# Swapping two first loads between two queues, and a new hand-written order for the first 668 of 1502 steps, in a packed-attention and gated-convolution kernel

## The chip, the cores and the metric

One core of one Trainium2 chip runs the whole kernel. The metric is the device time of one execution in microseconds; lower is better. In the text PE is TensorE, DVE is VectorE, ACT is ScalarE, POOL is GpSimd and SP is SyncE, whose queue issues nearly all loads.

## What is computed

```python
def sm_attn(qq, kk, vv):
    s = scale * np.matmul(qq, kk.transpose(0, 1, 3, 2))
    a = np.exp(s - np.max(s, axis=-1, keepdims=True))
    a = a / (np.sum(a, axis=-1, keepdims=True) + 1e-09)
    return np.matmul(a, vv)
p_packed = sm_attn(p, k, v)               # 32 packed queries over 576 keys
out = sm_attn(q, p_packed, p_packed)      # 576 queries over the 32 packed rows
x = out.transpose(0, 2, 1, 3).reshape(8, 576, 512)
h = np.maximum(x @ w_in, 0.0)             # 512 -> 1024
conv_out = conv3(h, conv_w)               # depthwise, 3 taps along the sequence
return h * sigmoid(conv_out) @ w_out      # 1024 -> 512
```

There are 8 batches of 8 heads, 576 positions and a head width of 64. q, k, v and p are float32; w_in, conv_w and w_out come as float64 and are rounded to float32 on the chip.

## The kernel before

**Tiling.** Four heads of one batch are a group g, so there are 16 groups, two to a batch. For each group `attention(g)` is a chain of 21 steps: score of the packed queries (PE, step 0, L744), maximum (DVE), exp (ACT), transposes (PE, L894), their eviction `a1T`, product with v (PE, step 5, L902), scaling `pb` (ACT), a transpose and its eviction `ppT`, second score (PE, step 9, L744), then transpose, maximum, subtraction, exp, sum, reciprocal, product and transpose back (mostly DVE), and a split of the result into two parts, `hi` and `lo` (steps 19 and 20). `packed_weight(b, hf)` multiplies the packed rows with w_in (L1099). `ffn1(b, j)` for 8 slices j of the hidden width multiplies that with the attention weights (L1162, L1188), then come relu (ACT), the taps of the convolution, tanh and the gate (DVE and ACT, L1205 to L1247). `ffn2(m)` for 36 row tiles is the last product (L1315 in f32 for the first three tiles, L1368 in three products for the rest), eviction and store. The first two groups of both first batches have their keys and queries transposed on PE (`kT`, `qT`, L720) and evicted to SBUF; from group 4 on, a DVE transpose does that (L680).

**Loads.** `load_kq`, `load_v`, `load_weight` (eight tiles w0 to w7 of 1 MB) and `queries` (the packed queries: p0 in two parts, then p1 to p3) issue on SP's queue, in the order in which their steps stand. Keys of groups 0 to 3 come in runs of 4608 B; from group 4 on, in four DMAs of 128 B pieces (L660); p1 is four DMAs of 128 B pieces too (L855). Three transfers are issued by ACT instead: the first 640 columns of the first keys (L632), the rest of them and, before, the keys of group 1 (`more_keys`, L668 and L671). `hold` keeps SP's other loads back until the first of these has landed.

**Order.** `ORDER` is a string of two-digit stream numbers: `Flow.run` takes the next step of the named stream, so that it fixes the order on every engine. `Flow` holds a planner's costs; they decide nothing in the program but how many idle matmuls (`warm`, L298) are put on PE where the plan finds it empty, until the first step of `ffn2(2)` has been placed. `ON_DVE` and `ON_POOL` name the operations that go to DVE rather than ACT, and to POOL rather than DVE; `either`, `either_pool`, `copy` (L349 on DVE, L351 on ACT) and `tensor_tensor` (L341 on DVE, L344 on POOL) follow them.

Of the kernel before, what the change touches and what calls it, by code (L numbers as in the profile page):

```python
# [18 lines left out]


ORDER = (
    "007f3603076y34023636036y340504050a040506050a70057001343a066z05056z350c34050e36340534050c3b0h0c053b0d0505340c7672"
    "3b0h7209360c050b050505080d713c36050j3b0b0c0c710c0c0j0c05050j0l3d3q053q0g770c0j3q0c0o0k0c3d3q3e0c0i0j3d0o0i0c0c73"
    "3d73740c3s740c3f3q3t3g3q3q0c0c3f780c3t3s3s0f3q3h3f3s0m0n3t3t0k3f793h3u3s0q3t3i3r0j3r0q3t3h0s0q3r3s0r3u3t0j3r3u3u"
    "0r370j0j3s0q0j0q3t0j0q3k3u0q0p3t3u3s0z3s0p753j3h0q3v0q7a753j3u3w0q3v3r3w3j0j3j400j3m0q5y370q3w3u3r0q3v0v405z3r3u"
    "3v603w3r5z5y3x3l7b603l0j3v0q3x3l373v3o403l0j0x0q3x400j0t3w3w3v0q0j0j0q0x5z5y0q123y0x3n0j3y3w0j3y3x3n3y3x60600x7c"
    "3n3y3z0x3z3z5y0j3n1441143p0q410x163x3z0u0q5z413x0y3p60605y0q7d143y3p190y15423z1d5z5z101e3y3j3l421142433z413p0w42"
    "43433z420x425y4444443l4342435z433n1445455y0x3j144515433n46605y441y0x456046464438440x4561451b46446046140x1b14465z"
    "0x471b3p45605y474846476113141g3p494847486149485z491761141b1b49485y1k484747614949486147496161616118141i0x4a141i62"
    "611i621c4b1b62621462621c1j140x630x380x4a1i62621b1b3862141i1b0x624a1i0x1j631a1z0x5z1n1r1b0x62141p626414141p636363"  # L30
    "141f1b0x634b63631b141i4b14631l141i631b4c1b1p4c641b4c1u631q4d1p4d4e1p1i644c1b1h4c4e4d4c1i1q1w1p644d651w1b1m1w644c"
    "4d4e1i251s4d1b4f1i1p4e4d4e4e646364641i641p211w644e654f4g1b1i4f1o1b1i1x4h4f4g641t6565644h1i1i1b4h651w4g4k1p4h4f23"
    "4g4k1i1p1x231w1p4f66651w6565234h4g4f4h4h1w1w4k1i4g6523651i234i6565661i4i1p4i1v284i4j66664j4g4i4j4i2a4l1p1w231w2a"
    "662a4m4i4n4j4j1p4j661p664m664j66664o1w4n4m666724672a244m1p6861391p671p4n1p23674n674o2k23674l2a6767674m4l4m204m4o"
    "4n4p4o232c2b4n66674p4n4q671w262a68391w222f232b4q394p4o4u4q274q4o2j4o234q2a692h2h694q2m1w684u1p4q4p6868681w1p4r4p"
    "4r1w2h68684u682d68682i4s4p2h4s294r4s2a691w6969692a4p692h234t4t2e68694t4s4r69694r2o1w4s4v4t6a6a2o2a692q2h1w6a2i4s"
# [27 lines left out]
class Flow:  # L64
# [98 lines left out]
    def transfers(self, step, at):  # L163
        issue, delay = self.ISSUE[step.engine]
        issue = step.issue or issue
        slow = 0
        for _ in range(step.parts):
            if step.engine == "SP":
                at = max(at, self.flights.pop(0))
            at += issue  # L170
            if self.hiccup and self.data >= self.hiccup:
                self.data += 600
                self.hiccup = 0
                slow = 500
# [48 lines left out]
def tile_packed_attention_conv_gate(  # L223
# [29 lines left out]

    F64_REBIAS = 2.0**-112
    PE_LO = 2
    ON_DVE = {"gh510", "hi0", "hi1", "hi12", "kT00", "kT05", "kT25", "kT30", "qT00", "relu34", "relu76", "tap00", "tap01", "tap21", "tap40", "tap41", "tap42", "tap44", "tap46", "tap53", "tap56", "tap57", "tap60", "tap61", "tap64", "tap65", "tap67", "tap70", "tap72", "tap73", "tap74", "tap75", "tap77", "x140", "x180", "x230", "x270", "x280", "x310", "x340", "x90"}
    ON_POOL = {"add00", "add01", "add10", "add41", "add51", "add61", "add70", "add71", "lo0", "lo10", "lo11", "lo7", "mul10", "mul12", "mul14", "mul2", "mul3", "mul4", "mul5", "mul6", "mul7", "mul9", "sub10", "sub11", "sub15", "sub2", "sub3", "sub4", "sub5", "sub7", "sub8", "sub9", "xl100", "xl110", "xl280", "xl30", "xl320", "xl330", "xl350", "xl50", "xl60", "xl70", "xl80"}
    COLD = 7
    F1F = ()
    F2F = 3  # L260
# [335 lines left out]
    def load_v(g):  # L596
        b, gg = divmod(g, NG)
        yield Step(
            "SP",
            (2350 if g < 2 else 2200) if g < APART else 2800,  # L600
            after=held(g),
            take=["v"],
            sets=[("v", g)],
            parts=2 if g < APART else 1 + HG,
            late=(300 if g >= APART else 1500) * (g > 3),
            issue=620 * (g >= APART),
        )
# [13 lines left out]
        nc.sync.dma_start(out=t[128 - TAIL :, :, SV, :], in_=src[:, 128 * SV :].rearrange("h r d -> r h d"))  # L621

    def load_kq(g, name, src):
        b, gg = divmod(g, NG)
        if by_block(g):
            i = g + (NG if name == "q" else 0)
            after = ready("kT", i - 3) if g < NG and i >= 3 else []
# [9 lines left out]
            after = after + held(g)  # L637
            parts = HG if name == "q" and quad(g, "q") and g % NG else 1
# [819 lines left out]
```

## Time and profile before

| | |
|---|---|
| median of three runs | 393.4 us (393.32, 393.40, 395.52) |
| the profiled execution | 393.78 us |
| its span, first to last instruction | 391.8 us |
| granted TensorE clock, mean | 1.00 |

The 2.0 us between span and time lie around the first and the last instruction. All times in the rows are counted from the start of the span.

### The profile page before, as it was taken

What the parts mean: (1) busy time and instruction counts of PE and PEld (TensorE: products, weight loads), DVE (VectorE), ACT (ScalarE), POOL (GpSimd) and SP (SyncE); (2) the same over time, 40 slices, a digit from 0 to 9 for tenths busy, and PEclk for the clock granted to TensorE, in tenths of its full rate; (3) what the DMA queues carried; (4) which work ended last, traced back from release to release, by engine and by line L of the source; (5) the groups of instructions that cost most, each with busy time, mean ns of one, the idle gap of its engine ahead of it and who ended that gap; (6) DMA issues with size and microseconds to landing.
All of it is one profiled execution on the core that took longest, in us unless ns stands there. A gap on an engine that the chain in (4) does not pass through costs nothing.

```text
span 391.8 us, 8179 instructions
## 1 busy us (share of the span) xinstructions
PE 386.2 (99%) x3299; PEld 308.4 (79%) x3299; DVE 331.6 (85%) x494; ACT 245.0 (63%) x403; POOL 73.8 (19%) x58
## 2 busy tenths in 40 slices
PE   8999999999999999999999999999999999999996
PEld 7667665769678887878787897898797879898886
DVE  3699899999989999999999989799987897987010
ACT  2999989988658776675846364673546554444211
POOL 2140332202532442051120103000001100200420
PEclk9999999999999999999999999999999999999999
DMA  8999899989599808998555134001001100000211
GB/s 270 376 392 270 189 306 143 192 154 184 113 163 158 186 5 181 183 163 149 121 88 142 35 87 89 0 28 54 28 2 54 54 28 27 28 0 28 80 54 56
DMA packets 157542, 47.62 MB, mean 122 GB/s; under 512 B 145460, under 2 KB 148788, under 8 KB 157504
## 3 DMA queue, kind: packets, MB, share of 16 engines
q1 hardware_dynamic: 157040, 45.89, 49.6%
q10 hardware_dynamic: 432, 1.18, 0.8%
q8 instruction: 26, 0.43, 0.5%
q14 instruction: 12, 0.10, 0.1%
q0 software_dynamic: 32, 0.02, 0.0%
HBM read 37.64 MB, written 9.44 MB: 120 GB/s over the span
## 4 chain that ended last, share of the span: by engine, by line
PE 90%; DVE 4%; DMA 3%; ACT 1%; SPq 1%; issue 0%; ACTq 0%; DVEq 0%
PE fo L1368 41%; PE big L1188 24%; PE sm L1368 4%; PE big L744 4%; PE big L1315 4%; PE big L1099 3%; PE sm L902 2%; DMA k<-in_k_dram 2%; PE big L894 2%; PE fo L1315 2%; DMA hgt<-in_k_dram 1%; PE fo L1274 1%; PE sm L1274 1%; PE big L720 1%; DVE w_in_sb L341 1%; DVE tmp L459 0%
## 5 line engine op out<-in xcount | busy, mean ns | idle before, releaser
L1368 PE MATMUL fo<-wo_hi,xhi 128*128 128x512 f32 x232 | 93.4, 402 | 0.0
L1368 PE MATMUL fo<-wo_hi,xlo 128*128 128x512 f32 x232 | 90.8, 391 | 0.0
L1368 PE MATMUL fo<-wo_lo,xhi 128*128 128x512 f32 x232 | 90.5, 390 | 0.0
L1205 ACT ACTIVATE hbuf<-big 128x576 f32<-128x576 f32 x62 | 40.2, 654 | 46.3 <-PE big L1188 46.0
L1237 DVE SCALAR_TENSOR_TENSOR hgt<-hbuf,cw,hgt 128x576 f32<-128x576 f32 x64 | 53.4, 843 | 4.6 <-ACT hgt L1235 4.3
L1188 PE MATMUL big<-a2hi,ghi 128*128 128x288 f32 x244 | 55.3, 308 | 0.0
L1245 ACT ACTIVATE hgt<-hgt 128x576 f32<-128x576 f32 x64 | 43.4, 685 | 17.7 <-DVE hgt L1241 17.5
L1368 PEld LDWEIGHTS fo<-wo_hi,xhi 128*128 128x128 f32 x232 | 43.5, 188 | 11.2 <-issue 1.4
L1188 PE MATMUL big<-a2lo,ghi 128*128 128x288 f32 x244 | 52.3, 296 | 0.0
L1188 PE MATMUL big<-a2hi,glo 128*128 128x288 f32 x244 | 52.3, 295 | 0.0
L1241 DVE SCALAR_TENSOR_TENSOR hgt<-hbuf,cw,hgt 128x576 f32<-128x576 f32 x64 | 51.1, 810 | 0.5
L1368 PEld LDWEIGHTS fo<-wo_hi,xlo 128*128 128x128 f32 x232 | 43.6, 188 | 9.7
L1247 DVE SCALAR_TENSOR_TENSOR hgt<-hgt,hbuf 128x576 f32<-128x576 f32 x64 | 47.3, 752 | 3.2 <-ACT hgt L1245 2.8
L1368 PEld LDWEIGHTS fo<-wo_lo,xhi 128*128 128x128 f32 x232 | 43.6, 188 | 7.1
L1188 PEld LDWEIGHTS big<-a2hi,ghi 128*128 128x128 f32 x244 | 41.2, 189 | 6.2 <-issue 1.9
L344 POOL TENSOR_TENSOR xlo<-hgt,xhi 128x1024 fp32r<-128x1024 f32 x11 | 28.0, 2544 | 93.9 <-ACT xhi L351 38.2
L1383 ACT COPY o<-fo 128x512 f32<-128x512 f32 x30 | 17.5, 584 | 35.7 <-PE fo L1368 27.9
L1188 PEld LDWEIGHTS big<-a2lo,ghi 128*128 128x128 f32 x244 | 39.2, 189 | 0.0
L1188 PEld LDWEIGHTS big<-a2hi,glo 128*128 128x128 f32 x244 | 39.1, 188 | 0.0
L1235 ACT ACTIVATE hgt<-hbuf,cw 128x576 f32<-128x576 f32 x42 | 32.4, 777 | 2.8 <-DVE hbuf L1203 2.3
L344 POOL TENSOR_TENSOR s<-s,mx 128x576 f32<-128x576 f32 x10 | 14.3, 1434 | 102.2 <-DVE hgt L1241 58.5
L351 ACT CAST xhi<-hgt 128x1024 fp32r<-128x1024 f32 (+1 forms) x28 | 26.5, 952 | 9.2 <-PE fo L1368 4.0
(138 smaller groups left out, 609.1 us busy)
## 6 DMA issues: line engine op xcount, KB each, us to landing
out_dram<-o SPq DMA_DIRECT2D x35, 256.0 KB, 2.3
k<-in_k_dram SPq DMA_DIRECT2D x48, 144.0 KB, 3.6
q<-in_q_dram SPq DMA_DIRECT2D x48, 144.0 KB, 3.4
v<-in_v_dram SPq DMA_DIRECT2D x40, 128.0 KB, 3.0
v<-in_v_dram SPq DMA_DIRECT2D x6, 512.0 KB, 10.6
hgt<-in_moe_w_in_dram SPq DMA_DIRECT2D x3, 1024.0 KB, 11.8
hgt<-in_moe_w_out_dram SPq DMA_DIRECT2D x3, 1024.0 KB, 8.4
hgt<-in_q_dram SPq DMA_DIRECT2D x2, 576.0 KB, 7.0
```

Of the source, the lines that this page charges most:

```text
L344: added = nc.gpsimd.tensor_tensor(**kw)
L351: nc.scalar.copy(out=out, in_=in_)
L1188: nc.tensor.matmul(out=t[:, hf, :SH], lhsT=w[:, gg, js], rhs=x[:, hf * SH : (hf + 1) * SH], start=n == 0, stop=n == (1 if b in F1F else 3) ...
L1205: nc.scalar.activation(out=inner, in_=t[:, :, :SH], func=AF.Relu, scale=0.5)
L1235: nc.scalar.activation(out=d, in_=h[:, 1 : S + 1], func=AF.Copy, scale=cw[:, NJ + j : NJ + j + 1])
L1237: nc.vector.scalar_tensor_tensor(out=d, in0=h[:, 0:S], scalar=cw[:, j : j + 1], in1=d, op0=ALU.mult, op1=ALU.add)
L1241: nc.vector.scalar_tensor_tensor(out=d, in0=h[:, 2 : S + 2], scalar=cw[:, 2 * NJ + j : 2 * NJ + j + 1], in1=d, op0=ALU.mult, op1=ALU.add)
L1245: nc.scalar.activation(out=d, in_=d, func=AF.Tanh)
L1247: nc.vector.scalar_tensor_tensor(out=d, in0=d, scalar=1.0, in1=h[:, 1 : S + 1], op0=ALU.add, op1=ALU.mult)
L1315: nc.tensor.matmul(out=t, lhsT=src[:, c, :], rhs=w32[c // 2][:, c % 2, :], start=c == 0, stop=c == NJ - 1)
L1368: nc.tensor.matmul(out=t, lhsT=x[:, c, :], rhs=w[:, c % 2, :], start=c + i == 0, stop=c == NJ - 1 and i == 2)
L1383: nc.scalar.copy(out=o, in_=t)
```

## The change

**Two loads.** `K1_FIRST` becomes False. ACT's third transfer is now the queries of group 0 (576 KB) where it was the keys of group 1 (576 KB); the other one of the two goes on SP's queue.

**Order.** `ORDER` is replaced in its first 668 steps. The same steps stand there in another order, and the last 834 are equal. In it the loads come like this (k2 is the keys of group 2, and so on):

```
before  ACT: k0, rest of k0, k1
        SP:  p0a q0 v0 w0 k2 p0b q1 v1 w1 k3 q2 w2 w3 v2 v3 q3 w4 k4 p1 w5 k5 w6 w7 v4 k6 q4 ...
after   ACT: k0, rest of k0, q0
        SP:  p0a k1 k2 v0 p0b w0 q1 v1 w1 k3 w2 q2 w3 v2 p1 v3 w4 q3 w5 k4 w6 k5 w7 v4 q4 k6 ...
```

On PE, the first steps are (att0.5 is step 5 of `attention(0)`, pw `packed_weight`, p0a and p0b the packed queries' transposes, second halves of transposes left out):

```
before  kT0 p0a att0.0 qT0 kT1 att0.3 att0.5 att1.0 att0.7 att0.9 kT2 att1.3 p0b qT1 att2.0 att1.5 att1.7 att1.9
        pw0 att2.3 kT3 qT2 ffn1(0,0) ... att3.5 qT3 att3.7 ffn1(0,3) ffn1(0,4) att3.9 pw0 pw1 ffn2(0) ...
after   kT0 p0a qT0 att0.0 kT1 att0.3 att1.0 att0.5 kT2 att0.7 p0b att0.9 att1.3 att2.0 qT1 att1.5 att2.3 att1.7 att1.9
        pw0 kT3 att3.0 qT2 ffn1(0,0) ... att3.5 ffn1(0,3) ffn1(0,4) qT3 att3.7 ffn2(2) pw0 att3.9 pw1 ffn2(0) ...
```

**Engines.** From DVE to ACT go the evictions kT05, kT25 and kT30, the casts hi0 and hi1, and the taps tap01 and tap21; from ACT to DVE pT0, pT2, kT15, kT35, gh001, a1T2 and tap02 (the first digit is the group or batch). From DVE to POOL go add11, add31 (halves of the rounding of w1 and w3) and lo4; from POOL to DVE add41 and xl80.

**Planner.** Its costs of loads are set anew, and a load in small pieces now holds the planned queue.

```diff
+    AHEAD = 2100
...
+            if step.issue:
+                at = max(at, self.data - self.AHEAD)
...
-    K1_FIRST = True
+    K1_FIRST = False
...
+        yield Step("SP", ..., sets=[("wd", i)], late=600 * (i in (5, 6)))
...
-            late=(300 if g >= APART else 1500) * (g > 3),
+            late=(100 if g >= APART else 600) * (g > 3),
...
-        yield Step("SP", 3450, take=["kq"], sets=[(name, g)], parts=4, late=700, issue=830)
+        yield Step("SP", 3450, take=["kq"], sets=[(name, g)], parts=4, late=-100, issue=810)
...
-            late=0 if i < 2 else 2500,
+            issue=550,
+            late=900 * (i >= 2) - 300 * (i == 1),
```

## Rows read from the trace of the kernel before

**Rows 1.** Page, part 1: engine, busy us (share), instructions.

```profile
PE 386.2 (99%) x3299; PEld 308.4 (79%) x3299; DVE 331.6 (85%) x494; ACT 245.0 (63%) x403; POOL 73.8 (19%) x58
```

**Rows 2.** Busy time of each engine in six stretches, with clock and DMA.

```profile
core 0: us, PE busy (x) PEld busy (x) DVE busy (x) ACT busy (x) POOL busy (x), PEclk, DMA share, GB/s
4.43:27.31 22.88, 22.49 (x291) 15.31 (x291) 16.34 (x32) 17.12 (x35) 5.28 (x4) 1.00 1.04 377
27.31:43.28 15.97, 15.59 (x227) 12.52 (x226) 15.79 (x29) 15.97 (x28) 0.00 (x0) 1.00 0.91 240
43.28:68.49 25.21, 25.15 (x214) 13.40 (x214) 24.17 (x40) 23.25 (x35) 9.55 (x8) 1.00 0.97 229
68.49:98.34 29.85, 29.85 (x224) 22.97 (x222) 29.84 (x40) 27.33 (x44) 5.40 (x3) 1.00 0.95 176
98.34:149.18 50.84, 50.84 (x592) 39.85 (x599) 49.17 (x78) 35.98 (x63) 21.45 (x13) 1.00 0.66 132
149.18:391.77 242.59, 238.94 (x1753) 201.29 (x1737) 195.60 (x278) 124.08 (x201) 30.01 (x17) 1.00 0.30 68
```

**Rows 3.** Chain that ended last, unhindered steps: start us, us, line, matmuls.

```profile
169.03 0.70 PE sm L902 x40
169.73 0.65 PE big L744 x16
170.38 0.86 PE big L1099 x16
...
179.03 1.60 PE big L1188 x12
180.64 0.55 PE big L894 x5
```

**Rows 4.** PE's costliest lines in 4.43 to 27.31: the idle matmuls.

```profile
L298 PE MATMUL idle<-zeros 128*128 128x512 f32 x15 | 5.5, 443 | 0.0
```

**Rows 5.** DMA issues from 0.5 to 7.5 us: KB each, us to landing.

```profile
hgt<-in_k_dram ACTq DMA_DIRECT2D x1, 576.0 KB, 4.6
hgt<-in_q_dram SPq DMA_DIRECT2D x1, 576.0 KB, 3.9
...
hgt<-in_moe_w_in_dram SPq DMA_DIRECT2D x1, 1024.0 KB, 7.3
...
v<-in_v_dram SPq DMA_DIRECT2D x1, 512.0 KB, 5.7
```

**Rows 6.** Timeline of PE and POOL, 4 to 28 us: start us, us, what.

```profile
11.62 0.77 PE L902 MATMUL sm<-v,a1T 128*32 128x64 f32 x40
...
13.88 0.71 PE L744 MATMUL big<-qT,ppT 64*32 64x288 f32 x16
...
22.37 1.43 POOL L344 TENSOR_TENSOR a2lo<-a2t,a2hi 128x576 fp32r<-128x576 f32 x1 [0.56 <-DVE a2hi L349]
...
27.31 0.54 PE L1162 MATMUL big<-a2hi,ghi 128*128 128x288 f32 x2
```

**Rows 7.** DVE's groups by shape up to 100 us: operations that change engine.

```profile
L341 DVE CUSTOM_DVE_ANT_0 w_in_sb<-tmp 128x1024 uint16<-128x1024 uint16 x5 | 3.4, 689 | 0.0
...
L349 DVE COPY kT<-big 128x640 f32<-128x640 f32 x2 | 1.6, 820 | 4.2 <-PE big L720 4.2
...
L349 DVE COPY kT<-big 128x512 f32<-128x512 f32 x2 | 1.4, 682 | 0.0
L1231 DVE TENSOR_SCALAR hgt<-hbuf,cw 128x576 f32<-128x576 f32 x2 | 1.0, 522 | 0.0
L349 DVE CAST a2hi<-a2t 128x576 fp32r<-128x576 f32 x2 | 0.9, 460 | 0.1
```

**Rows 8.** Timeline of SP's queue, 29 to 44 us: issuing instructions.

```profile
29.36 11.56 SPq L660 DMA_DIRECT2D k<-in_k_dram  x4
40.97 2.20 SPq L855 DMA_DIRECT2D p<-in_p_dram  x4
43.27 0.43 SPq L418 DMA_DIRECT2D stage<-in_moe_w_out_dram  x1
```

**Rows 9.** Waits of DVE and ACT: us in total, times, longest.

```profile
DVE pT L861 <- DMA p<-in_p_dram: 1.0, 1, 1.0
...
ACT tmp L455 <- DMA stage<-in_moe_w_out_dram: 0.7, 1, 0.7
```

**Rows 10.** DMA issues from 40.9 to 43.7 us: KB each, us to landing.

```profile
p<-in_p_dram SPq DMA_DIRECT2D x4, 64.0 KB, 2.5
...
stage<-in_moe_w_out_dram SPq DMA_DIRECT2D x1, 1024.0 KB, 5.7
```

More of the change, by code (lines that the diff above doesn't have):

```diff
@@ L21 @@
 ORDER = (
[L22 to L31, printed above, removed]
@@ L32 @@
-    "4d4e1i251s4d1b4f1i1p4e4d4e4e646364641i641p211w644e654f4g1b1i4f1o1b1i1x4h4f4g641t6565644h1i1i1b4h651w4g4k1p4h4f23"
-    "4g4k1i1p1x231w1p4f66651w6565234h4g4f4h4h1w1w4k1i4g6523651i234i6565661i4i1p4i1v284i4j66664j4g4i4j4i2a4l1p1w231w2a"
+    "007f36020334073403366y0e01046y34363634053a0434050a05347070050a090806343c6z05060c0c056z050h05360l0c36050h35050d05"
+    "3b0d053e3b720c72050j0b0g0c763g3b050j0j710b05050c0k05050c0j3b710k050c0c050c3d3q0f050j373q0c0c770c0o3d743d740c0c0c"
+    "0c0c3q3q3d0o0q0c3f0q0i780c0i0q3s3f0c3s3q3f3s3t3q3h3s3t3f0r3t733s0r3h0m3i3s793h3s3q3t0j3q3r730q0n3u3t0j3r0q3t0j3t"
@@ new lines @@
+    "0j3k3u3r3u0j0q3s3t3u373s3r3t3j3h0j3v3w7a3v0q0j3j0s0p0q3u3j3m3j3v0q3u75370p3u60753r3v3w0j0q3r0q400q3u3r3v0z3u3o3w"
+    "605y5z403r3w0q3v3l0v5y407b3x5z3l0t403v0q3l3w3l0j0q0j0q0j3y3x0x0q3w3n3y0j3w0j603z0x5y3y0q120x7c0j0j603y3n3y0x5z5z"
+    "0y3p3x0u0j0y3z0x3y3n3z3x143n160q140q410x3p41143x3y5y0x5z157d600q413z3p0w3l3x3j3x3p425y190x42420x3z5z424143433z43"
+    "5z143l42423z43425y60101d43113n14431k44153n4344454445455y3j3p444544464546465y14460x0x1b4660446014145z45611b464446"
+    "45471b475y614847131g3p4860491461484738170x491c6147491848476161496048611b6148615z49614947145y5z1b48491462610x4a38"
@@ L34 @@
+    "0x621i4b141c140x1i1b0x38620x1a4a6262631b621b1i62621i620x141i1j1b4a1e0x631j1n621414141i621r0x1b1p63141b63630x6363"
+    "1l1f621p1p1u1p634b1b6314141b1i1q141s1m4b1p63641i641h4c1i1b1b4c4c1q1b1b4d1w4c4d1i654c1y4d1p631p1i4e1b1i1t644e631i"
+    "4e1b1w4d4e4c4d1i4c1w4e4d64646464641w1p644f4e644d4f4e2164641p4g651o1i1z651w4f4g4h1b4g4f4f1x654h231p1x4k1w654g6565"
+    "65651i661i254h4g1w4g1p1i231p1b4g231i4k23654f4h664f4h1w651w23654h4k1i4h1p1i4i664i4i4j281v664i4j4i4j4i2a4l1w231w2a"
     "662a4m4i4n4j4j1p4j661p664m664j66664o1w4n4m666724672a244m1p6861391p671p4n1p23674n674o2k23674l2a6767674m4l4m204m4o"
@@ L255, in tile_packed_attention_conv_gate @@
     PE_LO = 2
-    ON_DVE = {"gh510", "hi0", "hi1", "hi12", "kT00", "kT05", "kT25", "kT30", "qT00", "relu34", "relu76", "tap00", "tap01", "tap21", "tap40", "tap41", "tap42", "tap44", "tap46", "tap53", "tap56", "tap57", "tap60", "tap61", "tap64", "tap65", "tap67", "tap70", "tap72", "tap73", "tap74", "tap75", "tap77", "x140", "x180", "x230", "x270", "x280", "x310", "x340", "x90"}
-    ON_POOL = {"add00", "add01", "add10", "add41", "add51", "add61", "add70", "add71", "lo0", "lo10", "lo11", "lo7", "mul10", "mul12", "mul14", "mul2", "mul3", "mul4", "mul5", "mul6", "mul7", "mul9", "sub10", "sub11", "sub15", "sub2", "sub3", "sub4", "sub5", "sub7", "sub8", "sub9", "xl100", "xl110", "xl280", "xl30", "xl320", "xl330", "xl350", "xl50", "xl60", "xl70", "xl80"}
+    ON_DVE = {"a1T2", "gh001", "gh510", "hi12", "kT00", "kT15", "kT35", "pT0", "pT2", "qT00", "relu34", "relu76", "tap00", "tap02", "tap40", "tap41", "tap42", "tap44", "tap46", "tap53", "tap56", "tap57", "tap60", "tap61", "tap64", "tap65", "tap67", "tap70", "tap72", "tap73", "tap74", "tap75", "tap77", "x140", "x180", "x230", "x270", "x280", "x310", "x340", "x90"}
+    ON_POOL = {"add00", "add01", "add10", "add11", "add31", "add51", "add61", "add70", "add71", "lo0", "lo10", "lo11", "lo4", "lo7", "mul10", "mul12", "mul14", "mul2", "mul3", "mul4", "mul5", "mul6", "mul7", "mul9", "sub10", "sub11", "sub15", "sub2", "sub3", "sub4", "sub5", "sub7", "sub8", "sub9", "xl100", "xl110", "xl280", "xl30", "xl320", "xl330", "xl350", "xl50", "xl60", "xl70"}
     COLD = 7
@@ L414, in load_weight @@
         after = after + [("kh", 0)] * (i < 3)
-        yield Step("SP", (2700, 2700, 2750, 2900, 3000, 3600, 3600, 4200)[i], after=after, sets=[("wd", i)])
+        yield Step("SP", (2700, 2700, 2750, 2900, 3000, 3600, 3600, 4200)[i], after=after, sets=[("wd", i)], late=600 * (i in (5, 6)))
         if src.dtype != F32:
```

## The prediction

> **What bounds the kernel now.** I began with the busy shares of the page [rows 1]: PE is busy for 386.2 of 391.8 us, at a granted clock of 1.00 throughout [rows 2]. That share hides waiting, because a matmul counts as busy up to its modelled end, so I laid PE's steps by their starts against the order and read the busy times by stretch [rows 2]. The cuts are PE's own steps: 4.43 is the first transpose of keys, 27.31 the first ffn1, and 149.18 the step att9.9, where the equal tail of the two orders begins. The chain in undisturbed places gives what a step costs [rows 3]: 1.60 us for an ffn1 of 12 matmuls, 0.70 for a product with v, 0.65 for a score, 0.55 for five transposes.
>
> With these unit costs PE has some 15.5 us of work in the first stretch of 22.88 us, so about 7 us there are lost. Fifteen idle matmuls fill part of that [rows 4]; the other loss is invisible waiting. In that stretch DVE and ACT are busy for 16.34 and 17.12 us, neither of them full, while the DMA share is 1.04 at 377 GB/s [rows 2]. So the start is bound by the arrival of data together with the latency of one chain, attention of group 0: product with v at 11.62, second score at 13.88, last split at 22.37, ffn1 at 27.31 [rows 6].
>
> From 27.31 to 43.28 PE's steps add up to some 13.6 to 14.5 of 15.97 us, so 1.5 to 2.4 are lost. Here ACT is busy for 15.97 and DVE for 15.79 us: both are full, and POOL does nothing [rows 2]. From 43.28 to 68.49 PE has some 24 of 25.2 us of work and loses 1.2. From 68.49 to 149.18 it loses about 1 us, most of it at changes between tiled and whole-array matmuls, which any order has. From 149.18 to the end the program is the same in both kernels: 242.6 us that the change can't touch. What can be won is thus a part of 7 + 2 + 1.2 us, and of the 7 us most is the latency of one chain.
>
> **The change, part by part.**
>
> *First loads.* ACT's third transfer, issued at 1.75, landed 4.6 us later, at 6.35; the queries on SP, issued at 4.31, landed 3.9 us later, at 8.2 [rows 5]. Both are 576 KB, so the swap exchanges the two landings: queries at about 6.4, keys of group 1 at about 8.2. In the kernel before PE transposes the queries from 8.67 on; now it can do so at 6.4, in place of two idle matmuls before the first score. The first score doesn't come earlier, since it waits for an eviction (second half of the keys) that moves to ACT, behind the first conversion of the taps, whose data land at about 6.5. I take 0 here (bounds -0.5 to +0.3).
>
> The Trainium skill (DMA: Bandwidth & Descriptors, "Issuing engines are not separate DMA queues") says that loads issued from several engines run on the same 16 DMA engines and interleave, so that only issue time is saved. By it this part alone is worth nothing, and the sum would be 0 as taken.
>
> *Order of the next loads.* The keys of group 2, 576 KB, now go ahead of v0 and w0. At 377 GB/s [rows 2] that is 1.56 us. v0 landed 5.7 us after its issue at 4.71, so at 10.4, and w0 7.3 us after 5.95, so at 13.25 [rows 5]; they now land near 12.0 and 14.8. The product with v stood at 11.62 [rows 6], so it goes to 12.1 to 12.3, and behind it now stand a transpose of keys and the queries' second part: the second score comes at about 14.5 instead of 13.88. By w1 the same bytes have been sent, and nothing later in this stretch moves. The chain of group 0 has 13.4 us from the second score to ffn1 [rows 6], of which only some 9.9 are its own (22.37 + 1.43 - 13.88); so a part of the 0.6 is taken up. The bounds are -2.0 (the evictions pT0, pT2 and kT15, which move to DVE while it idles, and earlier scores of groups 1 and 2, free ACT and PE) and +1.6 (the whole delay of v0). I take +0.3, nearest to the 0.6 that the rows give for the chain.
>
> *Engines.* Between 25 and 43 us, DVE loses an eviction of 640 columns (0.82), two halves of the rounding (2 x 0.69), a cast (0.46) and a tap (0.52), in all 3.18 us. It gains one half of rounding (0.69), two evictions of 512 columns (2 x 0.68) and a tap (0.52), in all 2.57 us [rows 7]. The net is -0.6 us of 15.79, and the two halves go to POOL, which stood empty [rows 2]. ACT, as full as DVE, takes over what DVE gave up and comes out about 0.2 us heavier. As one engine gains and the other doesn't, I take -0.3 of the -0.6 (bounds -1.0 and +0.3). The other exchanges lie in the first stretch, where neither engine is full, or after 98 us, where PE alone is: 0. That is covered by DVE's 1.7 us of idle time there [rows 2]; without that cover the 1.1 us of one split would show.
>
> *p1 and w5.* Before, four pieces of the keys of group 4 hold SP's queue from 29.36 to 40.92; p1 could be issued only at 40.97 and w5 at 43.27 [rows 8]. DVE stood still for 1.0 us waiting for p1 and ACT for 0.7 us waiting for w5 [rows 9], in the stretch where PE loses 1.2. Now p1 stands ahead of v3, and w5 ahead of k4. Both waits go. What is late next: v3, w4 and q3, pushed back by p1's 256 KB. By its bytes at 377 GB/s that is 0.7 us; by its landings (four pieces issued in 2.2 us, 2.5 us each to land [rows 8, 10]) up to 2.4; I take 1.5. v3 then lands at about 36.4, used before at 37.9 and now a little earlier; q3 at about 41, and its transpose now stands behind ffn1(0,3) and ffn1(0,4), at 41 to 42: both just in time. So of the 1.2 us that PE loses there I give back 0.5 (bounds -1.2, all of it, and +1.0, if v3 or q3 is late by a piece).
>
> The Trainium skill (DMA: Bandwidth & Descriptors, "Specifications") asks for at least 512 B a descriptor for line rate and calls what lies below a read-modify-write. That speaks against p1 ahead of v3. By it the delay is the longer one, 2.4 us, and this part would come to about 0 instead of -0.5. No row shows p1 beside large loads.
>
> **Sum** against the profiled execution of 393.78: 0 + 0.3 - 0.3 - 0.5 = -0.5, so 393.3 us. The median of the runs shown lies 0.4 under that execution; against the median the forecast is 392.9 us.
>
> **The rivals.**
>
> *Start shortened.* The 7 us of the first stretch are partly the search's to win: with queries at 6.4 and the first scores of groups 1 and 2 earlier, ffn1 could start 2 us earlier, and all of the 1.5 us or so that the middle stretches can give comes back too. For it speaks that DVE has 6.5 idle us in the first stretch [rows 2]; against it, that w1 and all loads behind it land no earlier. Time: 393.4 - 3.5 = 389.9.
>
> *v0 late* (slower). The product with v of group 0 waits for v0 behind k2, and w0 with it. If a1T is ready before v0 has landed, each tenth of delay goes into the chain of group 0, and PE has nothing else before ffn1. It decides from the point where v0 lands after about 11.6. The full price is 1.6 us, and with p1's pieces in front of v3 the same happens once more, up to 1.0. Time: 393.4 + 2.3 = 395.7. For it speaks the DMA share of 1.04; against it, that the new order puts att1.0 before att0.5.
>
> *It does nothing.* By the rule on issuing engines, as a mechanism of this kernel: the DMA engines are full up to 43 us, the same bytes pass, and the waits removed fall into slack of a PE that is full from 43 us on. Time: 393.4.
>
> **How the numbers follow.** Forecast 0.5, start shortened 0.2, v0 late 0.2, nothing 0.1. The predicted time is 392.9. The forecast's own bounds, with every term at one end together, would be 388.7 and 396.1; not all terms go one way, so the likely low end is 389.6, near the first rival's time, and the high end is 396.2, past the second's, which also takes in a spread of 2 us like that of the runs shown. One per cent, 3.9 us, is about what a measurement of this kernel can tell from no change: below 389.5 lies somewhat under half of the first rival and a little of the forecast, 0.10; above 397.3 a third of the second, 0.07; between them 0.83.
>
> **What would show it.** Right: queries transposed before 7 us, no DVE wait for p, no ACT wait for w_out, first ffn1 within 1 us of 27.3, step att9.9 at 148 to 149.5. A first ffn1 at 25.5 or earlier speaks for the first rival; a wait of the product with v for its data for the second. The forecast is wrong if att9.9 stands outside 146 to 151.5, or if the equal tail takes other than 242.6 us.

## The result, and the profile after

The changed kernel takes **396.57 us** (median of 14 runs, 394.73 to 398.28), the kernel before 393.4 (392.82 to 395.52): a ratio of 1.0073, interval 1.0059 to 1.0087. That is 3.2 us slower and just outside the predicted range of 389.6 to 396.2. The profiled execution took 396.24 us, its span is 394.4. Line numbers of the changed kernel are 3 or 4 higher than those of before (L744 is now L747, L902 is L906, L298 is L301).

Busy time by stretch, cut at the same PE steps as [rows 2] (columns as there):

```profile
4.33:29.03 24.70, 23.28 (x309) 15.77 (x308) 17.52 (x36) 18.02 (x35) 5.34 (x5) 1.00 1.04 367
29.03:43.21 14.18, 13.94 (x206) 11.67 (x205) 13.34 (x23) 13.13 (x22) 2.54 (x2) 1.00 0.92 271
...
99.34:151.63 52.29, 51.35 (x591) 39.67 (x593) 49.03 (x75) 37.78 (x66) 19.74 (x13) 1.00 0.94 153
151.63:394.37 242.74, 239.09 (x1753) 201.23 (x1745) 196.43 (x279) 124.13 (x201) 28.63 (x16) 1.00 0.34 67
```

The equal tail takes 242.74 us, where it took 242.59. The clock is 1.00 in both. So the loss lies ahead of att9.9, which starts at 151.63 in place of 149.18. Counting each step at its unit cost [rows 3], PE loses 9.7 us ahead of its first ffn1 (8.1 before, by the same count), 1.7 from ffn1(2,0) on to att9.9 (0.5 before), and in between 4.6 (4.9 before): 1.6 and 1.3 us lost, 0.3 won. These losses are of one execution of each kernel; the first ffn1, at 27.31 in that of before, starts at 27.4 to 28.3 in six other kernels whose PE has the same order up to it. The stretches in between don't hold the same steps in both orders (206 matmuls against 227 in the second), so their lengths are not to be compared.

**The early loss.** Timeline of the first 16 us, PE, then ACT, then DVE (start us, us, what; in brackets the idle time before and what ended it):

```profile
7.82 0.74 PE L723 MATMUL big<-ident,hgt 128*128 128x128 f32 x5 [1.01 <-DMA hgt<-in_q_dram]
8.49 0.71 PE L747 MATMUL big<-kT,pT 64*32 64x288 f32 x16
...
12.54 0.72 PE L747 MATMUL big<-kT,pT 64*32 64x288 f32 x16
13.18 0.77 PE L906 MATMUL sm<-v,a1T 128*32 128x64 f32 x40
...
15.31 0.72 PE L747 MATMUL big<-qT,ppT 64*32 64x288 f32 x16
...
7.53 0.31 ACT L371 ACTIVATE s<-s 24x128 f32<-24x128 f32 x1 [4.01 <-DMA s<-in_moe_conv_w_dram]
7.75 0.56 ACT L354 COPY kT<-big 128x512 f32<-128x512 f32 x1
...
10.31 0.74 ACT L886 ACTIVATE a<-big,nm 128x576 f32<-128x576 f32 x1 [1.78 <-DVE nm L882]
...
8.60 0.82 DVE L352 COPY qT<-big 128x640 f32<-128x640 f32 x1 [0.51 <-PE big L723]
9.34 0.27 DVE L378 CUSTOM_DVE_ANT_0 cw_raw<-s 24x256 uint16<-24x256 uint16 x1
9.54 0.74 DVE L882 TENSOR_REDUCE nm<-big 128x1 f32<-128x576 f32 x1
```

The first score and the exponential in the kernel before, from the same view:

```profile
7.45 0.72 PE L744 MATMUL big<-kT,pT 64*32 64x288 f32 x16
...
9.07 0.75 ACT L882 ACTIVATE a<-big,nm 128x576 f32<-128x576 f32 x1 [1.59 <-DVE nm L878]
```

The reader is to see four places where a step of the chain of group 0 stands behind one that isn't of that chain. PE has the queries' transposes ahead of the first score and waits 1.01 us for them; ACT has the conversion of the taps ahead of the second half of the first keys and waits 4.01 us for its data. The first score starts at 8.49, before at 7.45. DVE has the queries' eviction and a gather for the taps ahead of the maximum; with that, the exponential starts 1.24 us later than before (10.31 against 9.07), 1.04 of it from the late score. PE has the score of group 1 (12.54) ahead of the product with v, which starts at 13.18 where it was 11.62 [rows 6]. The second score is then at 15.31 in place of 13.88. `a1T` was evicted by 12.90, so the score of group 1 holds the product by some 0.3 us here: most of its 1.56 us come from the first score. The data of v0 landed at 12.34, so in this execution it isn't v0 for which the product waits.

Timeline of PE, then one row of ACT, up to the first ffn1:

```profile
25.16 0.50 PE L1131 MATMUL big<-ghi,minus 128*128 128x256 f32 x2
25.50 1.99 PE L301 MATMUL idle<-zeros 128*128 128x512 f32 x8
27.86 0.72 PE L747 MATMUL big<-kT,pT 64*32 64x288 f32 x16 [0.36 <-ACT kT L354]
28.51 0.77 PE L723 MATMUL big<-ident,q 128*128 128x128 f32 x5
29.03 0.51 PE L1166 MATMUL big<-a2hi,ghi 128*128 128x288 f32 x2
...
27.00 0.81 ACT L354 COPY kT<-big 128x640 f32<-128x640 f32 x1
```

From 25.5 to 27.86 PE has nothing but idle matmuls: the score of group 3 stands next in its order, and the eviction of its keys comes on ACT behind the conversion of w1. The inputs of the first ffn1 itself were ready at 27.2.

**The loads.** SP's queue in the timeline (start us, us that the issue held it, what):

```profile
21.05 10.69 SPq L859 DMA_DIRECT2D p<-in_p_dram  x4
31.84 0.44 SPq L614 DMA_DIRECT2D v<-in_v_dram  x1
...
33.59 0.56 SPq L421 DMA_DIRECT2D hgt<-in_moe_w_out_dram  x1
34.20 0.46 SPq L654 DMA_DIRECT2D q<-in_q_dram  x1
...
35.23 11.80 SPq L663 DMA_DIRECT2D k<-in_k_dram  x4
```

And from the waits of ACT between 4 and 60 us (in all, times, longest):

```profile
ACT tmp L458 <- DMA hgt<-in_moe_w_out_dram: 1.1, 1, 1.1
```

Issuing p1's four transfers now holds SP for 10.69 us; issued behind the keys of group 4 they took 2.2 [rows 8]. v3, w4 and q3, which were issued between 21.8 and 28.7, follow only at 31.8 to 34.2. The wait of DVE for p1 [rows 9] is gone, but w4 lands at 41.3 (before 39.2) and ACT waits for it.

**A store.** SP, ACT and PE near 130 us:

```profile
125.64 3.82 SPq L663 DMA_DIRECT2D q<-in_q_dram  x4
129.56 5.55 SPq L1392 DMA_DIRECT2D out_dram<-o  x2
...
134.14 0.59 ACT L1387 COPY o<-fo 128x512 f32<-128x512 f32 x1 [1.90 <-DMA out_dram<-o]
...
134.78 0.50 PE L1372 MATMUL fo<-wo_hi,xhi 128*128 128x512 f32 x1 [0.93 <-ACT o L1387]
```

Row tile 5 was evicted at 123.67, but its store stands behind two loads in 128 B pieces and is issued at 129.56. Until it has landed, ACT has no output buffer and PE no bank. Not every execution with this store order waits: the profile of the run "Late half" below has no such wait, its eviction starts at 133.84. No step of the prediction had looked at this place.

### The profile page after: what moved, and what is told of

Same layout as the page of the kernel before. It is cut to its first block, busy times and chain, and to the rows that moved or that the text cites. A ratio compares the mean times of both kernels' runs of the same rounds, so it can differ in the third digit from the quotient of the medians.

```text
span 394.4 us, 8189 instructions
## 1 busy us (share of the span) xinstructions
PE 386.6 (98%) x3304; PEld 308.9 (78%) x3304; DVE 332.4 (84%) x493; ACT 244.9 (62%) x403; POOL 72.4 (18%) x59
## 4 chain that ended last, share of the span: by engine, by line
PE 86%; DMA 5%; ACT 4%; DVE 3%; issue 1%; SPq 0%; ACTq 0%
PE fo L1372 40%; PE big L1192 22%; PE sm L1372 4%; PE big L747 4%; PE big L1319 4%; PE big L1103 4%; PE sm L906 2%; DMA hgt<-in_moe_w_out_dram 2%; PE fo L1319 2%; PE big L898 2%; DMA hgt<-in_q_dram 2%; DMA out_dram<-o 1%; ACT tmp L520 1%; PE big L723 1%; PE fo L1278 1%
## 5 line engine op out<-in xcount | busy, mean ns | idle before, releaser
L1209 ACT ACTIVATE hbuf<-big 128x576 f32<-128x576 f32 x62 | 40.4, 654 | 48.4 <-PE big L1192 48.3
L347 POOL TENSOR_TENSOR xlo<-hgt,xhi 128x1024 fp32r<-128x1024 f32 x10 | 24.9, 2486 | 95.5 <-ACT xhi L354 38.2
L1192 PEld LDWEIGHTS big<-a2lo,ghi 128*128 128x128 f32 x244 | 39.2, 188 | 0.0
L1239 ACT ACTIVATE hgt<-hbuf,cw 128x576 f32<-128x576 f32 x43 | 33.3, 780 | 2.9 <-DVE hbuf L1207 2.4
L347 POOL TENSOR_TENSOR s<-s,mx 128x576 f32<-128x576 f32 x10 | 13.4, 1338 | 115.9 <-DVE hgt L1245 58.5
```

The lines of the kernel that those rows point to most:

```text
L347: added = nc.gpsimd.tensor_tensor(**kw)
L1192: nc.tensor.matmul(out=t[:, hf, :SH], lhsT=w[:, gg, js], rhs=x[:, hf * SH : (hf + 1) * SH], start=n == 0, stop=n == (1 if b in F1F else 3) ...
L1209: nc.scalar.activation(out=inner, in_=t[:, :, :SH], func=AF.Relu, scale=0.5)
L1239: nc.scalar.activation(out=d, in_=h[:, 1 : S + 1], func=AF.Copy, scale=cw[:, NJ + j : NJ + j + 1])
```

## The experiments

Diffs of the order are written with the names of the steps; ratios are to the kernel before on the same chip, 1% is 3.9 us. Other steps stay as they are.

### Single parts on the kernel before

**Two loads swapped.**

```diff
-    K1_FIRST = True
+    K1_FIRST = False
```

> The kernel before with only the swap of the two first loads (queries of group 0 on ACT's queue, keys of group 1 on SP's), its order kept. Theory A (the swap is harmless by itself; what costs is an order that needs the queries at once): the queries are not needed before 8.67 us and the keys not before 9.21, so the time stays at 393.4, within 0.4 us, even if the queries land at 7.7 as in the changed kernel. Rival B (the queries on ACT's queue always land late, and the late first stage is due to the swap itself): first ffn1 1 us or more after 27.3, time 394.5 or more.

393.91 us, ratio 1.0018 (1.0000 to 1.0036). The queries landed at 7.5, the first score is at 6.98, the second at 13.74. By the ratio the swap costs 0.7 us, with an interval from 0 to 1.4; the first ffn1 is at 27.35, as before. The rival, 1 us or more late there, is out.

**Keys of group 2 ahead.**

```diff
-SP: p0a q0 v0 w0 k2 p0b
+SP: p0a q0 k2 v0 w0 p0b
```

> The kernel before with that one part alone: the keys of group 2 go ahead of v0 and w0 on SP's queue, nothing else moved. Theory A: v0 lands 1.5 us or more later (12 or later), the product with v of group 0 waits for it (it stood at 11.6), time 394.4 to 395.5. Rival B: time 393.2 to 393.9, since the chain has slack behind it.

395.32 us, ratio 1.0043 (1.0030 to 1.0055): this one load costs 1.6 us. Timeline of PE, then ACT:

```profile
13.54 0.77 PE L902 MATMUL sm<-v,a1T 128*32 128x64 f32 x40 [1.51 <-DMA v<-in_v_dram]
...
10.73 0.70 ACT L351 COPY a1T<-big 128x640 f32<-128x640 f32 x1
```

In the order of before, a1T is evicted at 11.4 and PE stands still for 1.51 us until v0 has landed, at 13.4. The second score comes at 15.79, the first ffn1 at 29.97 (before 27.31), att9.9 at 151.15: of the 1.9 us by which the second score is late, nothing is taken up.

**p1 and w5 ahead.**

```diff
-SP: v2 v3 q3 w4 k4 p1 w5 k5
+SP: v2 p1 v3 q3 w4 w5 k4 k5
```

> The kernel before with one part of the change alone, the later loads: p1 issued ahead of v3, and w5 ahead of the keys of group 4; the steps on the engines stay where they are. Theory A (the prediction's term: the waits of DVE for p1 and of ACT for w5 go, 0.5 us gained, w4 and q3 just in time): 392.6 to 393.4, no wait of DVE for p. Theory B (p1's pieces hold the queue and w4 comes 2 us later than before, so that ACT waits for w_out instead): 393.5 to 394.6.

396.02 us, ratio 1.0067 (1.0048 to 1.0087): 2.6 us slower, where the prediction had put 0.5 faster. SP's queue in the timeline, then the waits of DVE, ACT and PE between 24 and 60 us, then the busy times of two stretches (columns as in [rows 2]; the last two are DMA share and GB/s):

```profile
21.66 10.87 SPq L855 DMA_DIRECT2D p<-in_p_dram  x4
...
34.61 0.39 SPq L418 DMA_DIRECT2D hgt<-in_moe_w_out_dram  x1
```

```profile
DVE tmp L459 <- ACT tmp L455: 3.3, 1, 3.3
...
ACT tmp L455 <- DMA hgt<-in_moe_w_out_dram: 2.3, 1, 2.3
...
PE big L720 <- DMA q<-in_q_dram: 1.5, 2, 1.3
```

```profile
30.00:32.00 2.00, 1.95 (x14) 1.81 (x14) 2.00 (x5) 2.00 (x4) 0.00 (x0) 1.00 0.83 153
32.00:34.00 2.00, 1.89 (x33) 1.25 (x39) 2.00 (x6) 2.00 (x4) 0.00 (x0) 1.00 0.39 58
```

From the same views of the kernel before, two stretches and the issue of v3:

```profile
32.00:34.00 2.00, 2.00 (x40) 1.09 (x38) 2.00 (x5) 2.00 (x4) 0.00 (x0) 1.00 1.05 397
38.00:40.00 2.00, 2.00 (x52) 1.91 (x53) 2.00 (x4) 2.00 (x5) 0.00 (x0) 1.00 0.38 70
```

```profile
21.79 4.09 SPq L611 DMA_DIRECT2D v<-in_v_dram  x1
```

The reader is to see the whole mechanism. While SP is held until 32.5, what had been issued runs out, and the transfer rate falls to 58 GB/s; before, the same two stretches had 308 and 397. q3 lands at 40.1 (36.1 before), w4 at 44.0 (39.2). PE waits for q3, ACT for w4, and DVE for ACT. The keys of group 4 come later too (their first piece at 48.4, before 39.7), and DVE waits 1.1 us for them. Before, the same hollow lay at 38 to 42 us (70 and 91 GB/s), behind w4, where only p1, w5 and those keys came late. A large load can be held as well: at the place where p1 now stands, the large part of v3 held SP for 4.09 us before. What p1 adds is the difference: w4 is issued at 34.61 in place of 28.68. The run doesn't part p1 from w5's move ahead of the keys.

**The same, p1 issued by POOL.**

```diff
-                nc.sync.dma_start(
+                (nc.gpsimd if i == 1 else nc.sync).dma_start(
```

> The kernel before with the later loads moved as in the run that came to 396.02 (p1 ahead of v3, w5 ahead of the keys of group 4), but p1's four transfers are issued by POOL, which has nothing to do there. Theory A (the price is that p1's issue holds SP's queue for 10.9 us, so that v3, q3 and w4 are issued late and the transfer engines run empty at 30 to 34 us): v3 is issued before 26 us, w4 lands before 40.7, time 393.0 to 394.0. Theory B (the small pieces cost the transfer engines the time itself, whoever issues them): w4 lands after 42 and the time is 395.0 or more.

394.45 us, ratio 1.0015 (1.0001 to 1.0030): 2 us of the 2.6 are back. POOL's timeline, then the same two stretches:

```profile
27.43 2.61 POOL L855 DMA_DIRECT2D p<-in_p_dram  x4
```

```profile
30.00:32.00 2.00, 2.00 (x16) 1.80 (x14) 1.97 (x5) 2.00 (x5) 0.04 (x1) 1.00 1.14 285
32.00:34.00 2.00, 1.98 (x24) 1.54 (x26) 2.00 (x6) 2.00 (x4) 0.00 (x0) 1.00 1.15 251
```

v3 was issued from 22.5 on and the rate stays above 250 GB/s. w4 lands at 41.4; landing and time lie between the two theories' numbers. The executions differ ahead of p1 already (w3 lands at 31.0 before, at 31.4 with p1 on SP and at 31.9 here), so w4 is better counted from the landing of w3: 8.2 us before, 12.6 with p1 on SP, 9.5 here. Of the 4.4 us that p1 costs w4 so counted, some 3.1 are the hold of SP's queue and 1.3 are left with the pieces themselves; that 1.3 is rough, since the same distance is 8.0 to 9.0 in three other runs that leave these loads alone. It is mostly the hold that cost PE.

**p1 ahead of the other small pieces only.**

```diff
-SP: w4 k4 p1 w5
+SP: w4 p1 k4 w5
```

> The kernel before with p1 issued ahead of the keys of group 4, behind w4; nothing else moves. Both are in pieces of 128 B, so the time in which they hold SP's queue is the same, only which of them comes first differs. Theory A (what costs is small pieces ahead of large loads; behind w4 nothing large is delayed): p1 lands near 41, DVE's wait of 1.0 us for it goes, the keys of group 4 land at 43.5 to 45, time 392.6 to 393.4. Theory B (p1 ahead costs wherever it stands): 394.0 or more.

394.29 us, ratio 1.0004 (0.9986 to 1.0023). DVE's wait for p1 went; in its place ACT waits 1.7 us for w5 in the profiled execution. No gain, no loss: p1 behind w4 delays nothing large.

**A candidate: all these pieces on POOL.** The order of before, keys of group 4 and p1 issued by POOL.

```diff
-                nc.sync.dma_start(
+                (nc.gpsimd if name == "k" and g == 4 else nc.sync).dma_start(
...
-                nc.sync.dma_start(
+                (nc.gpsimd if i == 1 else nc.sync).dma_start(
```

> A candidate to beat both: the kernel before, with the order of the loads as it is, but the keys of group 4 and p1 (eight transfers in pieces of 128 B) issued by POOL, which does nothing between 24 and 44 us, in place of SP. Theory A (their hold on SP's queue, 29.4 to 43.2 us, is what makes w5 late and leaves the transfer engines at 70 to 90 GB/s at 38 to 42 us): w5 is issued by 31 us and lands before 45, the waits of DVE for p and of ACT for w5 go, time 0.3 to 1.0 us below before. Theory B (PE gains nothing from these waits, or w4 and q3 come later because the pieces now run beside them): within 0.3 us of before, or slower by up to 1 us.

398.65 us, ratio 1.0116 (1.0096 to 1.0136): a plain miss. PE's waits, then a stretch:

```profile
PE sm L902 <- DMA v<-in_v_dram: 2.7, 1, 2.7
```

```profile
38.00:40.00 2.00, 0.79 (x17) 0.18 (x16) 2.00 (x5) 1.90 (x4) 0.00 (x0) 1.00 1.02 246
```

The engines are full at 246 GB/s: POOL's pieces now run beside v3, q3 and w4, and the large part of v3 lands at 41.4 in place of 34.5. It was issued at 22.6, and yet the first piece of the keys, issued by POOL at 28.1, landed ahead of it, at 36.1. On one queue the pieces wait their turn behind these. (The Trainium skill, DMA: Bandwidth & Descriptors, "Queues, rings and completion order", says that each transfer engine takes turns between the queues that have work for it; this run agrees.)

### Halves of the change

**Early half of the change.** The changed order and loads for its first 127 steps, up to its first ffn1; that of before behind it.

```diff
-ORDER: before
+ORDER: after, up to ffn1(0,0); then the steps left, as in before
```

> The other half: order, engines and first loads of the changed kernel up to its first ffn1 (127 steps), those of the kernel before for all behind. Theory A: first ffn1 at 29 to 31, time 395.5 to 397, with runs some 3 us apart. Rival B: time 394.2 or less.

396.60 us, ratio 1.0085 (1.0065 to 1.0105), first ffn1 at 31.14: this half alone costs as much as the whole change. But p1's load is among its steps, ahead of v3, and holds SP here too:

```profile
21.75 10.63 SPq L859 DMA_DIRECT2D p<-in_p_dram  x4
```

So the run doesn't part the early order on the engines from p1's hold.

**Late half.** The reverse, 116 steps of before first.

```diff
-ORDER: after
+ORDER: before, up to ffn1(0,0); then the steps left, as in after
```

> Order and engines of the kernel before up to the step before its first ffn1 (116 steps, and its first loads), those of the changed kernel for all steps behind. Theory A (what costs lies before the first ffn1: there the two profiles differ by 1.7 us, and the spread of the changed kernel's runs comes from its first loads): first ffn1 at 27.3 to 28.2, time 393.4 to 394.6, with a spread as small as before. Rival B (what costs lies behind: p1 ahead of v3, the late store of tile 5): first ffn1 near 27.5 but time 395.5 or more.

395.96 us, ratio 1.0051 (1.0032 to 1.0069). Here too p1 stands ahead of v3 and holds SP from 21.75 for 11.1 us, so both halves have that part of the change in them. The second score is at 13.83, but in PE's timeline:

```profile
27.49 1.64 PE L301 MATMUL idle<-zeros 128*128 128x512 f32 x6
29.06 0.71 PE L747 MATMUL big<-kT,pT 64*32 64x288 f32 x16
29.71 0.54 PE L1166 MATMUL big<-a2hi,ghi 128*128 128x288 f32 x2
```

The score of group 3 again holds the first ffn1, whose own inputs were ready at 25.5; PE had nothing but idle matmuls between the transposes ahead of that score, done at 27.7, and 29.06.

**Late half, ffn1 first.**

```diff
-PE: att3.0 ffn1(0,0)
+PE: ffn1(0,0) att3.0
```

> The order of before for the first 116 steps and that of the changed kernel behind them, as in the earlier hybrid (first ffn1 at 29.71 there, time 395.96), and now the first ffn1 ahead of the score of group 3. Theory A (in that hybrid the score of group 3 ahead of ffn1 was all of the loss): first ffn1 at 25.8 to 27.5 us, time 393.4 to 394.4. Theory B (the evictions on ACT and DVE are the bound behind the first ffn1 in the changed order): first ffn1 below 28 us and the time still above 395.2.

395.28 us, ratio 1.0051 (1.0032 to 1.0070); first ffn1 at 27.42. The ratio doesn't move.

**And p1 behind w5.**

```diff
-SP: p1 v3 w4 q3 w5 k4
+SP: v3 w4 q3 w5 p1 k4
```

> Order and loads of before for the first 116 steps, the changed order behind them with the first ffn1 ahead of the score of group 3 (395.28 in the run before) and now p1 behind w5. Theory A (p1's hold on the queue is what was left of the loss there): w4 lands before 40 us, the time is 393.0 to 394.0, near that of before. Theory B (the changed order of the middle stretches costs by itself): 394.5 to 395.4, with ACT or DVE waiting for each other between 27 and 45 us.

394.32 us, ratio 1.0019 (1.0009 to 1.0030), w4 at 38.0: p1's place was worth 1.3 us here, and what is left of the late half is 0.7, with the late store in it.

### Parts put back in the changed kernel

**First score ahead of queries and taps.**

```diff
-PE: qT0 att0.0        ACT: convw, second half of kT0
+PE: att0.0 qT0        ACT: second half of kT0, convw
```

> The changed kernel with two steps of its order moved: on ACT the eviction of the second half of the first keys goes ahead of the first conversion of the taps, and on PE the first score goes ahead of the queries' transposes. Theory A (the first score at 8.49 instead of 7.45 waits for two late landings, the queries at 7.68 and the taps at 7.51, and the whole chain of group 0 is late by that): first score at 7.3 to 7.6, first ffn1 at 28.0 to 28.4 instead of 29.03, time 395.4 to 396.0 (0.6 to 1.1 us off 396.6). Rival B (the chain is bound later, by the loads of w0 and w1 and by ACT): the first score comes earlier, the first ffn1 stays at 28.8 to 29.1, time 396.3 to 396.8.

397.59 us, ratio 1.0093 (1.0064 to 1.0123). First score at 7.89, second at 16.01: no gain. On DVE the maximum still stood behind the queries' eviction.

**Early store.**

```diff
-SP: q9 store(5)
+SP: store(5) q9
```

> The changed kernel with one step of its order moved: the store of row tile 5 goes on SP's queue right behind that tile's eviction, ahead of the queries of group 9, not behind them. Theory A (at 133.7 to 134.8 PE waits for an eviction that waits for the buffer of that store, which stood on SP behind eight DMAs of 128 B pieces): ACT's wait for the store (1.9 us) and PE's (0.9 us) go, and the time falls by 0.8 to 1.1 us to 395.5 to 395.8. Rival B (PE's wait only moves to the next step, or the loss is one of this one profile): time 396.3 to 396.8.

396.74 us, ratio 1.0080 (1.0059 to 1.0101). The loss behind ffn1(2,0) went from 1.3 to 0.1, yet the time didn't fall: in that execution the early stage lost 11.4 us, with an early program that is the changed kernel's own. There the product with v does wait for v0, which landed at 13.68:

```profile
13.82 0.77 PE L906 MATMUL sm<-v,a1T 128*32 128x64 f32 x40 [0.75 <-DMA v<-in_v_dram]
```

Whether the early store is worth anything stays open.

**p1 behind w5.**

```diff
-SP: p1 v3 w4 q3 w5 k4
+SP: v3 w4 q3 w5 p1 k4
```

> The changed kernel with the load of p1 (and the two DVE steps that use it) moved back behind w5 on SP's queue, ahead of the keys of group 4, so that v3, w4 and q3 are no longer behind its small pieces. Theory A (p1's pieces hold SP from 21 to 31.7 us and make w4 land at 41.3 instead of 39.2, on which the chain runs): w4 at 39.5 or earlier, ACT's wait for it (1.1 us) goes, time 395.6 to 396.2. Rival B (PE loses no more between 29 and 69 us than in the kernel before, so the place of p1 is worth nothing): 396.3 to 396.9.

396.32 us, ratio 1.0060 (1.0042 to 1.0077). w4 landed at 39.6; against 1.0073 no gain that these runs can tell.

**Keys of group 2 behind w0.**

```diff
-SP: k1 k2 v0 p0b w0     PE: kT2 att0.7 p0b att0.9
+SP: k1 v0 p0b w0 k2     PE: att0.7 p0b att0.9 kT2
```

> The changed kernel with the keys of group 2 moved back behind v0, p0b and w0 on SP's queue, and their transposes behind the second score of group 0. Theory A (these keys push v0 and p0b back, and the chain of group 0 waits for them): v0 lands at 10.4 to 11.5 instead of 12.3 to 14.1, second score at 14.2 to 14.8 instead of 15.3 to 16.0, time 395.2 to 396.0. Rival B (the early stage is late for another reason, such as the order of DVE and ACT): second score at 15 or later, or the first ffn1 still at 29 or later, time 396.3 to 397.

396.24 us, ratio 1.0066 (1.0053 to 1.0079). v0 landed at 10.8, and the second score stayed at 15.30: here the order on the engines holds it.

**ffn1 ahead of the score of group 3.**

```diff
-PE: att3.0 qT2 ffn1(0,0)
+PE: ffn1(0,0) att3.0 qT2
```

> The changed kernel with one PE step moved: the first ffn1 (first two groups, slice 0) goes ahead of the score of group 3 and the second part of the queries of group 2, which stand ahead of it in the changed order and wait there for the evictions of the keys of group 3. Theory A (this place in PE's order is what makes the first ffn1 late): the first ffn1 starts at 27.0 to 28.0 us instead of 29.03, step att9.9 comes about 1 us earlier, and the time is 395.2 to 395.9. Theory B (PE only exchanges one wait for another; what follows the first ffn1 needs the same evictions, and the middle stretches take the gain back): first ffn1 earlier, but att9.9 at 151.4 or later and the time within 0.4 of the changed kernel's 396.6.

395.64 us, ratio 1.0058 (1.0040 to 1.0077). First ffn1 at 27.05, att9.9 at 151.02: between the theories, 0.6 of the 2 us reach att9.9.

**Three parts together** (the last two and the early store).

```diff
-SP: k2 v0 p0b w0      PE: att3.0 ffn1(0,0)      SP: q9 store(5)
+SP: v0 p0b w0 k2      PE: ffn1(0,0) att3.0      SP: store(5) q9
```

> The changed kernel with three of its parts put back together: keys of group 2 loaded behind v0, p0b and w0 (their transposes behind the second score of group 0), the first ffn1 ahead of the score of group 3, and the store of row tile 5 right behind its eviction. Theory A (each is a cause, and one alone gains nothing since the next one holds the same stretch): the time falls to 393.2 to 394.6, about that of before. Theory B (the changed order of the chains of groups 0 to 2 on PE, ACT and DVE costs the time whatever is loaded when): the first ffn1 stays behind 28.5 us and the time between 395.6 and 396.8.

395.01 us, ratio 1.0040 (1.0026 to 1.0054): half of the loss is back, though each alone gained little.

**Four together** (p1 behind w5 as well).

```diff
-SP: p1 v3 w4 q3 w5 k4
+SP: v3 w4 q3 w5 p1 k4
```

> The changed kernel with four parts put back together: the three of the run before (keys of group 2 behind v0, p0b and w0; first ffn1 ahead of the score of group 3; early store of row tile 5), and p1 back behind w5, with the steps on DVE that use it. That run came to 395.01, and the later loads alone to 396.02. Theory A (two losses, each enough to hide the other: the early order and p1's hold on SP's queue): with both put back the time is 393.2 to 394.3, and w4 lands before 40.2 us. Theory B (the early order still costs by itself, whatever is loaded when): 394.7 to 395.4.

395.54 us, ratio 1.0049 (1.0036 to 1.0061), w4 at 38.5. p1 is worth nothing here; the second score is still at 15.26.

**Five: and the first 30 steps as before.**

```diff
-ORDER, engines: the first steps as in after
+ORDER, engines: the first 30 steps as in before
```

> The kernel with four parts put back (395.54 where before read 394.03, a ratio of 1.0049), and now a fifth: the first 30 steps in the order of before, with their engines. In it the first score and its maximum stand ahead of the queries' transposes on PE and of their eviction on DVE, and the second half of the first keys is evicted by DVE, not by ACT behind the conversion of the taps; the queries still come on ACT's queue. Theory A (the first score, 8.28 us there and 6.6 to 7.5 in kernels with the early order of before, is what is left of the loss): first score below 7.6 us, second score below 14.6, ratio to before 1.000 to 1.0025. Theory B (the loss lies in the order of the chains of groups 1 and 2 behind it): the first score early, but the first ffn1 still at 28 us or later and the ratio 1.0035 to 1.006.

395.82 us, ratio 1.0046 (1.0031 to 1.0061). PE, then ACT:

```profile
12.88 0.24 PE L534 MATMUL sm<-ident,cw_raw 24*128 24x24 f32 x1
13.05 0.71 PE L747 MATMUL big<-kT,pT 64*32 64x288 f32 x16
13.70 0.77 PE L906 MATMUL sm<-v,a1T 128*32 128x64 f32 x40
...
10.96 0.69 ACT L354 COPY a1T<-big 128x640 f32<-128x640 f32 x1
```

The first score is at 7.56, but a1T, evicted by 11.65, waits until 13.70 behind the taps' transpose and the score of group 1. The edit traded one hold for another, so it doesn't tell its theories apart.

## Why the prediction was wrong

Two things in the prediction failed. The first is the step **p1 and w5**: its measured price lies furthest outside its bounds, because it left out that issuing p1 holds SP's queue. The second is the start: **First loads** took the new order around them at 0, and **Order of the next loads** came out at the end of its bounds.

- *p1 and w5*: -0.5, with bounds of -1.2 and +1.0. By themselves, on the kernel before, they are +2.6. The step took p1's price from bytes and landings (0.7 to 2.4 us, 1.5 taken), and the pieces' own time fits that: some 1.3. What it left out is the hold: w4 came 4.8 us later there, some 3 of it because SP couldn't issue it (in the changed kernel v3, forecast for 36.4, landed at 37.2, and q3, for 41, at 42.7). The row that showed this was in the prediction's hands: the keys of group 4, in the same pieces, hold SP for 11.56 us [rows 8]. The step used it to say why p1 came late and not for what p1 would do in front of large loads. The Trainium skill's 512 B (DMA: Bandwidth & Descriptors, "Specifications"), weighed there and set aside, pointed the right way; the 2.4 us taken by it covers the pieces' own time but not the hold, which no sentence there gives.
- *Order of the next loads*: +0.3, with +1.6 as the upper bound. Alone it is +1.6. The step counted 13.4 us for the chain from the second score to ffn1 against 9.9 of its own, and let the difference take up half of the delay. The difference isn't slack: loads behind k2 come later too (w1 at 24.2 in place of 22.3), and the chain waits on ACT and DVE behind the weights' conversions.
- *First loads*: 0, with +0.3 as the upper bound. The swap by itself can't be told from 0 (0.7, interval 0 to 1.4). But the landing of 6.4 for the queries was one execution's: in the changed kernel they landed at 7.68, and in eight other kernels that keep the first issues of before, ACT's third transfer landed at 7.1 to 7.8 and never at 6.3. With the queries' transposes, their eviction and the taps set ahead, the order makes the first score 1.0 us late. The step saw the taps' conversion in front of the keys' eviction and priced it at nothing. What the early order costs without the keys of group 2 shows in two runs that both have p1 behind w5 and the first ffn1 ahead of the score: "Four together", with the early order of after, has 1.9 us left (ratio 1.0049), "And p1 behind w5", with that of before, 0.7 (1.0019).
- *Engines*: -0.3. Between the first ffn1 and ffn1(2,0) PE loses 0.3 us less in all, later loads included; no run takes this step by itself.
- *Rivals*: "v0 late" gave 395.7, the nearest time. Its mechanism is real by itself (1.51 us of wait for v). In the profiled execution of the changed kernel v0 isn't what is waited for; in that of the run with the early store, which has the same early program, it is, for 0.75 us. What the rival took as speaking against it, att1.0 ahead of att0.5, is no cover but a hold of the product with v: some 0.3 us in the changed kernel, and with the taps' transpose 2.0 with five parts put back. "Start shortened" and "it does nothing" are out, and the transfer engines aren't full up to 43 us, as the latter had it: at 38 to 42 us their share is 0.38 and 0.60.
- *What would show it*: DVE's wait for p went and the tail held, as said; the queries' transposes at 7.82, first ffn1 at 29.03 and att9.9 at 151.63 were outside the marks, and ACT's wait for w_out stayed.
- *Sum*: the upper bounds add up to 3.2 us, which from 393.4 gives 396.6 and not 396.1; the lower end, 388.7, does count from 393.4. That 396.57 lies at that end is no sign that the mechanism was right: one term alone came out far above its bound, and the parts don't add up.

**Why it isn't a sum.** k2 alone costs 1.6 us, p1 and w5 by themselves 2.6, the early half with k2 and p1 in it 3.3; the whole change costs 3.2. p1's place is worth 2.6 us (with w5's) on the kernel before, 1.3 with the early order of before, and nothing that can be told with the changed early order (ratio 1.0073 to 1.0060, and 1.0040 to 1.0049). That a late start hides late loads would fit this, and also that single parts put back gained little; no run shows it directly.

**What stays open.** With three, four or five parts put back 1.6 to 1.9 us are left; with the whole early order of before, 0.7. The second score is at 15.2 to 16.0 in nine kernels with the changed early order, and at 13.6 to 14.3 in nine with that of before, one of them with the two first loads swapped; which of the four holds costs most wasn't separated. The exchanges of engines and w5's place weren't run by themselves either. No version here beats the kernel before.

## What to carry to other kernels

A load in small pieces costs twice: its time on the transfer engines, and the time for which its issue holds the queue while there is a backlog. Large loads are held by a backlog too, but less here (4.09 us for the large part of v3, 10.87 for p1, at the same place). Price it by how long the row of the issuing engine says, and by what stands behind it there; place it behind the last large load that is needed soon. On a second queue the hold goes, but its pieces then take bandwidth from the loads beside them.

In a hand-written order, look on each engine for a step that waits for data and stands ahead of the chain which sets the stage's end. Idle time between the steps of a chain is slack only if none of its other inputs moves with the delay.

## What was not expected of the hardware

Issuing four transfers in 128 B pieces took SP 10.7 to 10.9 us with a backlog and 2.2 us without one, and POOL, on a queue of its own, 2.6 us at the same place in the order. Landings of one and the same early issue differ by up to 1.5 us between executions of programs whose first issues are equal (6.3 in one, 7.1 to 7.8 in eight others), about as much as the keys of group 2 ahead of v0 cost.
